# One K for the two lowest score levels, and the first block through two experts before the second

## The chip, the cores and the metric

The kernel runs on one core of one Trainium2 chip. The metric is device microseconds for one execution. TensorE, VectorE, ScalarE and GpSimd are abbreviated PE, DVE, ACT and POOL in the profile, and PEld is TensorE's load of stationary operands. SP is the engine whose queue issues most transfers.

## The reference

A gated linear attention recurrence on 4 batches, 8 heads, 768 tokens and 48 dimensions is followed by a mixture of 4 experts over all tokens, each with two layers (384 to 1024 to 384), weighted by normalised probabilities. All in float32:

```python
for t in range(S):                                   # S = 768, D = 48
    state = alpha[:, :, t, :, None] * state + np.einsum('bhd,bhe->bhde', k[:, :, t], v[:, :, t])
    y[:, :, t] = np.einsum('bhd,bhde->bhe', q[:, :, t], state)
x = y.transpose(0, 2, 1, 3).reshape(B * S, H * D)    # 3072 x 384
p = domain_probs / (domain_probs.sum(-1, keepdims=True) + 1e-09)
for e in range(4):
    out += p[:, e:e + 1] * (np.maximum(x @ w1[e], 0.0) @ w2[e])
```

## The kernel before

**Units and groups.** The tokens are cut into 24 units, each 128 tokens of one batch (`units`). Units 0 and 1 form group 0, then come groups of four units, and the last group has two. For each group all four experts are run over the group's tokens; a unit's place in its group is its slot. `up(gi, e, fc, slots)` is one of eight column tiles of expert e's first layer (line 790 for group 0, line 796 for the others) and `down(gi, e, slots, ...)` is the second layer (line 875). In this text (0, 1) stands for group 0 with expert 1.

**Group 0 works on plain float32 weights.** A matmul in plain float32 leaves two records in the trace. From group 1 on, float32r matmuls are used with the weights split into parts. The splits are made during group 0: `split_piece` (lines 261, 263, 264) rounds a piece on ScalarE, takes the rests on VectorE, and GpSimd's queue writes the parts to `kept` in DRAM (line 268), from where later groups load them. A list `making` says which pieces come next, and `background()` starts one at each of its calls, with at most four under way. Each expert has four pieces (NQ = 4) of 384 KB for each layer. The raw first-layer weights of experts 0 and 2 use one set of tiles, those of experts 1 and 3 another (`shared`); the next expert's are loaded at the middle of `up` of the present expert. The raw second-layer weights of group 0 are loaded into one part of the `hidden` tiles (hT).

**Attention of a unit.** `attention(u)` is a generator; each `yield` ends a step. The steps turn alpha, K and Q (AT, KT, QT: rows are the dimensions of head pairs, columns the 128 tokens). Up to unit 5 this is done on TensorE (`turned`, line 298), from unit 6 on (`in_runs`) by VectorE's transpose (line 499). The rows of the transposed tiles that hold no dimension are set to zero by a scale of 0 or 1 per row, held in the last column of `ident_all`; before, that is an activation on AT (line 503). Then come seven levels: at level li tokens are paired in blocks of m = 1, 2, 4, ... 64; the later block's Q is scored against the earlier block's K, with decay between them. For each level, `copy_q` (line 552, ScalarE, two copies of 64x256) writes the later blocks' Q into one of four tiles `qb`, with the two heads of a pair apart; `next_q` multiplies Q by decay in place (line 559) and joins decays (line 561); `next_k` copies half of K (line 570, ScalarE) and multiplies the other half (line 571). `products` makes a level's scores: 16 matmuls of 32 columns (line 579). `take` writes them into `near` through a mask (line 586). Levels 5 and 6 are `mid` (line 638) and `far` (line 633). Scores are copied to `lat` (lines 650, 653, 658), and `result` makes the unit's output `yps` (line 680). The state is updated through `sps` (line 717).

**Order.** The engines' order is written by hand. While the matmuls of the experts are emitted, `advance(cost)` moves a clock; `waiting` holds steps of units with the clock at which each is due, so the attention of later units stands between the matmuls of earlier ones. `deal()` spreads the steps of units 2 and later over the time by `BEATS`. Unit 0 has a function of its own (`first_unit`), which also runs unit 1's first three steps. Before, the first block, unit 0, goes through expert 0 alone (the loop with `up(0, 0, fc, slice(0, 1))`) while the rest of unit 1's attention is emitted; then unit 1 goes through expert 0, and both units through experts 1, 2 and 3 together.

Of the kernel before, what the change touches and what calls it, by code (L numbers as in the profile page):

```python
# [20 lines left out]
def kernel(  # L21
# [41 lines left out]
    P = 128  # L63
# [74 lines left out]

    blocks = [const.tile([P, NP, 2, HALF], F32, name=f"qb{i}") for i in range(4)]
    free = deque(blocks)  # L140

    def raw(u, nm):
        if nm == "v":
# [26 lines left out]

    def portions(gi, e):
        n = len(groups[gi])
        return [slice(1, n)] if gi == e == 0 else [slice(0, 3), slice(3, n)] if (gi, e) == (1, 0) else [slice(0, n)]

    fresh = lambda gi, e: gi == 1 or (gi, e) == (2, 0)

# [35 lines left out]
    def load_piece(l, i, beside=False, rest=False):  # L212
        if i >= E * NQ * LAST:
            return
        gi, k = divmod(i, E * NQ)
        e, c = divmod(k, NQ)
        if gi > l and not (l == 1 and fresh(gi, e)):
            if l == 0:
                w = wt[l][i] = wts.tile([P, 3, KC * QF], F32R, name="w1", bufs=AHEAD)
                nc.sync.dma_start(out=w.bitcast(F32), in_=kept[l][k])  # L220
                return
            w = second(rest)
            nc.sync.dma_start(out=w.bitcast(F32), in_=kept[l][k][:, 2:] if rest else kept[l][k][:, :2])
            wt[l].setdefault(i, []).append(w)
            return
        if l == 1 and gi == 0 and not beside:
            return
        if l == 0:

            if e == 0:  # L230
                shared[c] = second(True)[:, 0], second(False)[:, 1]
            w = shared[c][e % 2].bitcast(F32)
        else:

            if gi > 0:
                if c == 0:
                    shared["w2"] = hid.tile([P, NQ, KC * QF], F32, name="raw2", bufs=1)
                w = shared["w2"][:, c]
            else:
                w = hidden[c][:, 0].rearrange("p f n -> p (f n)")[:, :KC * QF].bitcast(F32)  # L240
        wt[l][i] = w
        if l == 0:
            nc.sync.dma_start(
                out=w.rearrange("p (c f) -> p c f", f=QF),
                in_=moe_w1[e].rearrange("(c p) f -> p c f", p=P)[:, :, c * QF:(c + 1) * QF])
        else:
            nc.sync.dma_start(
                out=w.rearrange("p (c d) -> p c d", d=DM),
                in_=moe_w2[e].rearrange("(c p) d -> p c d", p=P)[:, c * FPQ:(c + 1) * FPQ])
# [237 lines left out]
    def attention(u):  # L487
# [12 lines left out]

        if u >= in_runs:
            turn("a", AT)
            nc.scalar.activation(out=AT, in_=AT, func=ACT.Copy, scale=ident_all[:, P + QUAD:])
        else:
            nc.scalar.copy(out=AT, in_=turned(pair(ra)))
        after = u + 1 if u > 1 else len(units)
# [17 lines left out]
            own_terms()  # L524
        yield
        load(after, "k")
        if u >= in_runs:
            turn("q", QT)
            nc.vector.tensor_mul(QT, QT, AT)
        else:  # L530
            nc.vector.tensor_mul(QT, turned(pair(rq)), AT)
        if own_late:
            own_terms()
        yield
        load(after, "q")

        decs = [AT]
        KTs = [KT]  # L540
        qbs = []
        spread = lambda t, m: t.unsqueeze(3).broadcast_to([*t.shape, m])
        halved = lambda t: t.rearrange("p a (b two) -> p a b two", two=2)

        def copy_q(li):
            m = LEVELS[li]
            qv = halves(QT, m)[:, :, :, 1, :]
            qb = free.popleft()
            qbs.append(qb)
            for i in range(2):  # L550
                rows = slice(HD * i, HD * (i + 1))
                nc.scalar.copy(out=qb[rows, :, i, :].rearrange("p a (b r) -> p a b r", r=m),  # L552
                               in_=qv[rows])
# [10 lines left out]
        def next_k(li):  # L564
            m = LEVELS[li]
            old = new = halves(KTs[li], m)
            if li + 1 < len(LEVELS):
                KTs.append(keys())
                new = halves(KTs[-1], m)
                nc.scalar.copy(out=new[:, :, :, 1, :], in_=old[:, :, :, 1, :])  # L570
            nc.vector.tensor_mul(new[:, :, :, 0, :], old[:, :, :, 0, :],  # L571
                                 spread(halved(decs[li])[:, :, :, 1], m))

        def products(li, out):
            each = QUAD // 2
            for p in range(NP):
                for s in range(P // QUAD):
                    rows = slice(QUAD * s, QUAD * (s + 1))
                    nc.tensor.matmul(out[rows, 2 * p:2 * p + 2], lhsT=KTs[li][:, p, rows],  # L579
                                     rhs=qbs[li][:, p, :, each * s:each * (s + 1)], start=True, stop=True)  # L580
            free.append(qbs[li])

        def take(li, scores):
# [4 lines left out]
                mk.unsqueeze(1).broadcast_to([P, H, QUAD // (2 * m), m]),  # L588
                scores.rearrange("p a (b r) -> p a b r", r=m))

        def scores(n):
            return ps.tile([P, n, H, QUAD // 2], F32, name="sc", tag="sc")


        for li in range(3):
            copy_q(li)
            next_q(li)
            next_k(li)
            yield
        copy_q(3)  # L600

        nc.vector.tensor_mul(near, ident_all[:, P:P + QUAD].unsqueeze(1).broadcast_to([P, H, QUAD]),
                             dot.unsqueeze(2).broadcast_to([P, H, QUAD]))
        yield
        bank = scores(3)
        for li in range(3):
            products(li, bank[:, li])
        next_q(3)
        next_k(3)
        take(0, bank[:, 0])  # L610
        take(1, bank[:, 1])
        yield
        copy_q(4)
        next_q(4)
        next_k(4)
        take(2, bank[:, 2])
        yield
        copy_q(5)
        next_q(5)
        next_k(5)  # L620
        yield
# [1 line left out]
        if cb > 0:  # L623
            next_q(6)
        yield
        bank = scores(3)
        mid = bank[:, 2].rearrange("p (r i x) n -> p r i (x n)", i=2, x=2)
        far = ps.tile([P, NP // 2, 2, HALF], F32, name="far", tag="sc")

        for r in range(NP // 2):  # L630
            for n in range(P // QUAD):
# [3 lines left out]
        for r in range(NP // 2):  # L635
            for n in range(P // QUAD):
                s, p = n // 2, 2 * r + n % 2
                nc.tensor.matmul(mid[QUAD * n:QUAD * (n + 1), r], lhsT=KTs[5][:, p, HALF * s:HALF * s + QUAD],  # L638
                                 rhs=qbs[5][:, p, :, QUAD * s:QUAD * (s + 1)], start=True, stop=True)
        for li in (3, 4):  # L640
            products(li, bank[:, li - 3])
        free.extend(qbs[5:])
        take(3, bank[:, 0])
        take(4, bank[:, 1])
        next_k(6)
        yield
        parts = lat.rearrange("p (r s i) c -> p r s i c", s=2, i=2)
# [112 lines left out]
    def up(gi, e, fc, slots=None):  # L760
# [2 lines left out]
        begins, ends = lo == 0, hi == n  # L763
        c, f = divmod(fc, FPQ)
        i = first_piece(gi, e) + c
        if fc == 0 and begins:
            for k in range(NQ):
                hidden[k] = hid.tile([P, 2, FPQ, NT], F32R, name="hT", bufs=NQ)
        if gi == fc == 0 and begins:
            for k in range(NQ):  # L770
                load_piece(1, e * NQ + k, beside=True)
        beside = BESIDE[(gi, e) == (1, 0)]
        if fresh(gi, e) and fc in beside and begins:
            making.append(split_piece(1, first_piece(gi, e) + beside[fc]))
        if gi == 0 and e > 0 and fc in SPLIT_AT:
            making.append(split_piece(0, e * NQ + SPLIT_AT[fc]))
        if gi == 0 and e + 1 < E and fc == FCH // 2 and begins:
            for k in range(NQ):
                load_piece(0, (e + 1) * NQ + k)
        col = slice(f * P, (f + 1) * P)  # L780
        if gi > 0:
            w = wt[0][i].rearrange("p t (c f) -> p t c f", f=QF)[:, :, :, col]
        else:
            w = wt[0][i].rearrange("p (c f) -> p c f", f=QF)[:, :, col]
        parts = [hidden[c][:, part, f, lo:hi] for part in range(2)]
        whole = parts[1].bitcast(F32)
        one = ps.tile([P, NT], F32, name="one", tag="g", bufs=4)[:, :hi - lo]
        if gi == 0:
# [35 lines left out]
    def down(gi, e, slots, between):  # L824
# [1 line left out]

        first = first_piece(gi, e)
        tiles = range(FCH)
        if gi == e == slots[0] == 0:
            making.extend(split_piece(0, k) for k in range(NQ))  # L830
        if gi == 0 and e < E - 1 and slots[0] == (e == 0):
            making.extend(split_piece(0, first + NQ + k) for k in range(2))
        if gi == 0 and e == E - 1 and slots[0] == 1:
            making.extend(split_piece(1, first + NQ + k) for k in range(NQ // 2))
# [17 lines left out]
        for n, (slot, part, fc) in enumerate(steps):  # L852
# [12 lines left out]
                    load_piece(1, first + NQ + k)  # L865
            if n == begins[slot]:
                sums[slot] = ps.tile([P, DM], F32, name="ops", tag="g", bufs=4)
            h = hidden[c][:, :, f, slot * P:(slot + 1) * P]
            if part < 3:
                w = ws[c][part // 2].rearrange("p t (c d) -> p t c d", d=DM)[:, part % 2, f]  # L870
                h = h[:, part % 2]
# [96 lines left out]
    with tc.manual_schedule():  # L968
# [4 lines left out]
            for r in (early[nm], apart[nm]):  # L973
                nc.gpsimd.memset(r[:, :, D:], 0.0)
        nc.gpsimd.memset(lat, 0.0)
        for t in values + blocks:
            nc.gpsimd.memset(t, 0.0)
        for t in sts[:-1]:
            nc.gpsimd.memset(t, 0.0)
# [11 lines left out]
        def fill(times, n=P):  # L991
            for _ in range(times):
# [5 lines left out]
        nc.sync.dma_start(out=p_all, in_=moe_domain_probs.rearrange("(n p) e -> p n e", p=P))  # L998

        span = cost(0, 0, 0) * FCH / 2 + cost(1, 0, 0)  # L1000
        waiting.extend((span * (k + 1) / 15, u, runs[u])
                       for k, u in enumerate([1, 1, 1, 0, 1, 0, *[1] * 8]))
        for fc in range(FCH):
            up(0, 0, fc, slice(0, 1))
            if fc == FCH // 2:
                norm_probs()
            advance(cost(0, 0, 0) / 2)
        down(0, 0, [0], deque())
        while waiting:
            next(waiting.popleft()[2], None)  # L1010
        clock = 0.0
        waiting.extend((1.0 + k, 1, runs[1]) for k in range(2))
        waiting.extend(deal())

        for (gi, e), after in zip(tasks, [*tasks[1:], (None, None)]):
            pieces = portions(gi, e)
# [45 lines left out]
```

## Time and profile before

| what | value |
|---|---|
| median of 3 runs | 993.67 us (991.96 to 996.77) |
| profiled execution, its own time | 995.26 us |
| span of the profile | 993.5 us |
| mean granted TensorE clock | 0.993 |
| TensorE busy | 966.4 us (97%) |
| VectorE / ScalarE busy | 545.1 us (55%) / 468.5 us (47%) |
| HBM read, written | 219.69 MB, 42.47 MB |

The chain that ended last is 90% TensorE; the two layers of the experts (lines 875 and 796) make 40% and 37% of the span, the score products of line 579 make 3%. Group 0's experts run from 22.1 us to about 155 us, and the first expert matmuls of group 1 begin at 155.0 us. A busy TensorE in these tables is not TensorE at its peak, and some records of matmuls are missing, so that counts in short stretches can fall short.

### The profile page before, as it was taken

What the parts mean: (1) busy time and instruction counts of PE and PEld (TensorE: products, weight loads), DVE (VectorE), ACT (ScalarE), POOL (GpSimd) and SP (SyncE); (2) the same over time, 40 slices, a digit from 0 to 9 for tenths busy, and PEclk for the clock granted to TensorE, in tenths of its full rate; (3) what the DMA queues carried; (4) which work ended last, traced back from release to release, by engine and by line L of the source; (5) the groups of instructions that cost most, each with busy time, mean ns of one, the idle gap of its engine ahead of it and who ended that gap; (6) DMA issues with size and microseconds to landing.
All of it is one profiled execution on the core that took longest, in us unless ns stands there. A gap on an engine that the chain in (4) does not pass through costs nothing.

```text
span 993.5 us, 26117 instructions
## 1 busy us (share of the span) xinstructions
PE 966.4 (97%) x10988; PEld 860.4 (87%) x10988; DVE 545.1 (55%) x1217; ACT 468.5 (47%) x1106; POOL 47.1 (5%) x95
## 2 busy tenths in 40 slices
PE   8799979999999999999999999999999999999998
PEld 7677658989889889899899898898988999999998
DVE  4676668596866756556545545656666321131312
ACT  4676776584554654445454434555455313111111
POOL 2010000020110200000000000000000000000000
PEclk9999989999999999999999999999999999999999
DMA  9499996899999999978987968988797707272721
GB/s 207 150 336 325 312 356 194 239 315 324 384 305 338 350 311 339 329 275 298 342 256 265 331 221 300 366 273 260 269 312 274 269 2 287 94 288 93 282 99 49
DMA packets 168325, 263.86 MB, mean 266 GB/s; under 512 B 93040, under 2 KB 136432, under 8 KB 155920
## 3 DMA queue, kind: packets, MB, share of 16 engines
q1 hardware_dynamic: 160464, 219.79, 67.7%
q0 software_dynamic: 7296, 42.08, 10.6%
q8 instruction: 86, 1.41, 0.6%
q10 hardware_dynamic: 448, 0.32, 0.1%
q14 instruction: 31, 0.25, 0.1%
HBM read 219.69 MB, written 42.47 MB: 264 GB/s over the span
## 4 chain that ended last, share of the span: by engine, by line
PE 90%; ACT 3%; DMA 2%; DVE 2%; issue 1%; SPq 0%; POOL 0%; DVEq 0%; ACTq 0%; POOLq 0%
PE ops L875 40%; PE one L796 37%; PE yps L680 4%; PE sc L579 3%; PE one L790 2%; DMA w2r<-in_moe_w_dram 2%; PE tp L298 2%; PE far L633 1%; ACT qb L552 1%; PE sps L717 1%; DMA sq<-in_q_dram 1%; PE sc L638 0%; DVE AT L499 0%; PE idle L993 0%; ACT w L261 0%
## 5 line engine op out<-in xcount | busy, mean ns | idle before, releaser
L796 PE MATMUL one<-xT,w 128*128 128x512 f32 (+2 forms) x1512 | 346.9, 385 | 0.0
L796 PEld LDWEIGHTS one<-xT,w 128*128 128x128 f32 x1512 | 274.7, 188 | 52.9 <-issue 0.2
L875 PE MATMUL ops<-w,hT 128*128 128x384 f32 x1408 | 253.9, 338 | 0.0
L798 ACT ACTIVATE hT<-one 128x512 fp32r<-128x512 f32 (+3 forms) x200 | 109.1, 546 | 301.6 <-PE one L796 300.8
L875 PEld LDWEIGHTS ops<-w,hT 128*128 128x128 f32 x1408 | 243.3, 188 | 2.3 <-issue 0.2
L821 DVE SCALAR_TENSOR_TENSOR hT<-one,hT 128x512 fp32r<-128x512 f32 (+3 forms) x200 | 123.7, 626 | 129.4 <-ACT hT L798 128.9
L559 DVE TENSOR_TENSOR QT<-QT,AT 128x256 f32<-128x256 f32 x158 | 67.0, 424 | 153.7 <-ACT qb L552 152.6
L552 ACT COPY qb<-QT 64x256 f32<-64x256 f32 x322 | 130.7, 406 | 16.6 <-PE sc L579 6.6
L875 PE MATMUL ops<-w2r,hT 128*128 128x384 f32 x704 | 127.8, 337 | 0.0
L875 PEld LDWEIGHTS ops<-w2r,hT 128*128 128x128 f32 x704 | 122.2, 188 | 0.3 <-issue 0.2
L896 DVE SCALAR_TENSOR_TENSOR acc<-ops,p_all,acc 128x384 f32<-128x384 f32 x66 | 39.5, 613 | 73.9 <-PE ops L875 73.5
L571 DVE TENSOR_TENSOR KT<-KT,AT 128x256 f32<-128x256 f32 x161 | 67.3, 418 | 0.0
L570 ACT COPY KT<-KT 128x256 f32<-128x256 f32 x138 | 57.6, 417 | 3.3
L586 DVE COPY_PREDICATED near<-masks,sc 128x128 f32<-128x128 uint8 x115 | 40.8, 355 | 27.4 <-PE sc L579 25.8
L579 PEld LDWEIGHTS sc<-qb,KT 128*32 128x32 f32 x3680 | 37.7, 110 | 15.6 <-issue 10.3
L579 PE MATMUL sc<-qb,KT 128*32 128x32 f32 x3680 | 42.3, 198 | 7.1 <-ACT qb L552 3.6
L875 PE MATMUL ops<-hT 128*128 128x384 f32 x128 | 48.0, 522 | 0.0
L905 POOL DMA_DIRECT2D out_dram<-acc x22 | 11.9, 540 | 671.1 <-DVE acc L896 671.1
L561 DVE TENSOR_TENSOR AT<-AT 128x256 f32<-128x256 f32 (+1 forms) x138 | 39.0, 283 | 4.7
L875 PEld LDWEIGHTS ops<-hT 128*128 128x128 f32 x128 | 24.5, 203 | 15.1 <-issue 2.7
L658 ACT COPY lat<-near 32x256 f32<-32x256 f32 x92 | 36.9, 401 | 0.8
L680 PE MATMUL yps<-lat,rv 128*32 128x128 f32 x736 | 33.9, 279 | 2.1 <-ACT lat L658 2.1
(127 smaller groups left out, 783.1 us busy)
## 6 DMA issues: line engine op xcount, KB each, us to landing
w<-kept SPq DMA_DIRECT2D x80, 1152.0 KB, 7.6
w<-kept SPq DMA_DIRECT2D x60, 768.0 KB, 8.1
w2r<-kept SPq DMA_DIRECT2D x60, 384.0 KB, 7.5
kept<-w POOLq DMA_DIRECT2D x16, 1152.0 KB, 8.9
kept<-w POOLq DMA_DIRECT2D x16, 768.0 KB, 13.1
raw<-in_moe_w_dram SPq DMA_DIRECT2D x20, 384.0 KB, 13.1
hT<-in_moe_w_dram SPq DMA_DIRECT2D x16, 384.0 KB, 5.6
kept<-w2r POOLq DMA_DIRECT2D x16, 384.0 KB, 14.2
```

The source lines that it names most:

```text
L552: nc.scalar.copy(out=qb[rows, :, i, :].rearrange("p a (b r) -> p a b r", r=m), in_=qv[rows])
L559: nc.vector.tensor_mul(qv, qv, spread(dv[:, :, :, 0], m))
L570: nc.scalar.copy(out=new[:, :, :, 1, :], in_=old[:, :, :, 1, :])
L571: nc.vector.tensor_mul(new[:, :, :, 0, :], old[:, :, :, 0, :], spread(halved(decs[li])[:, :, :, 1], m))
L579: nc.tensor.matmul(out[rows, 2 * p:2 * p + 2], lhsT=KTs[li][:, p, rows], rhs=qbs[li][:, p, :, each * s:each * (s + 1)], start=True, stop=True)
L586: nc.vector.copy_predicated(near.rearrange("p a (b two r) -> p a b two r", two=2, r=m)[:, :, :, 1, :], mk.unsqueeze(1).broadcast_to([P, H, ...
L680: nc.tensor.matmul(yps[QUAD * j:QUAD * (j + 1), c, :], lhsT=lhsT, rhs=rhs, start=begins, stop=ends)
L796: nc.tensor.matmul(one, lhsT=w[:, part, kc], rhs=x_part(gi, part % 2, kc)[:, lo:hi], start=(part == 1 and kc == 0), stop=(part == 0 and kc ...
L798: nc.scalar.activation(out=parts[0], in_=one, func=ACT.Relu)
L821: nc.vector.scalar_tensor_tensor(out=low, in0=x, scalar=0.0, in1=top.bitcast(F32), op0=ALU.max, op1=ALU.subtract)
L875: nc.tensor.matmul(sums[slot], lhsT=h, rhs=w, start=(n == begins[slot]), stop=(n == ends[slot]))
L896: nc.vector.scalar_tensor_tensor(out=acc, in0=part, scalar=scale, in1=acc, op0=ALU.mult, op1=ALU.add)
```

## The change

Two things are changed.

In `attention`, the mask is applied to Q instead of A: AT is no longer scaled, the copies of Q for level 0 take the scale, and Q times A becomes one instruction with the scale in it. Level 0 is scored with the unscaled Q of the odd tokens against K after level 0's decay, which is the K that level 1 uses too; so level 0's K is updated in place, with no copy. The Q of levels 0 and 1 goes into one new tile `odd`, and one set of 16 matmuls of 64 columns (QUAD = 32 for each of the two heads) makes both levels' scores. Levels 2 and 3 join them in the first scores; the second scores hold `far`, `mid` and level 4 in one bank. The copies of Q for a level are issued at the end of the step before. The number of steps is the same.

In the order of group 0, unit 0 goes through expert 0 and then expert 1, while the rest of unit 1's attention, and the first steps of `deal()`, stand between; then unit 1 goes through experts 0 and 1; experts 2 and 3 run over both. For that, expert 1's raw second-layer weights are loaded in the middle of `up` of expert 0 into the tile `raw2`; expert 1's hidden values for group 0 go into the second half of expert 0's `hidden` tiles; the splits and the load of expert 2's first-layer weights move to the pass in which the expert is last used by `up`.

```diff
 def portions(gi, e):
-        return [slice(1, n)] if gi == e == 0 else ...
+        return [slice(1, n)] if gi == 0 and e < 2 else ...
 # load_piece, second-layer weights
-            if gi > 0:
+            if gi > 0 or e == 1:
 # attention
         if u >= in_runs:
             turn("a", AT)
-            nc.scalar.activation(out=AT, in_=AT, func=ACT.Copy, scale=ident_all[:, P + QUAD:])
...
+        def copy_pairs(src, li):
+            m = LEVELS[li]
+            to = odd.rearrange("p a i (s l b r) -> p a i s l b r", l=2, b=EACH // m, r=m)
+            of = halves(src, m)[:, :, :, 1, :].rearrange("p a (s b) r -> p a s b r", b=EACH // m)
+            for i in range(2):
+                rows = slice(HD * i, HD * (i + 1))
+                nc.scalar.activation(out=to[rows, :, i, :, li], in_=of[rows], func=ACT.Copy,
+                                     scale=pads[rows] if li == 0 and u >= in_runs else 1.0)
 # next_k
-            if li + 1 < len(LEVELS):
+            if li == 0:
+                KTs.append(KT)
+            elif li + 1 < len(LEVELS):
 # steps: Q, then levels 0 to 4
+        if u >= in_runs:
+            turn("q", QT)
+            copy_pairs(QT, 0)
+        else:
+            plain = turned(pair(rq))
+            nc.vector.tensor_mul(QT, plain, AT)
+            copy_pairs(plain, 0)
...
+        if u >= in_runs:
+            nc.vector.scalar_tensor_tensor(out=QT, in0=QT, scalar=pads, in1=AT, op0=ALU.mult, op1=ALU.mult)
+        next_q(0)
+        next_k(0)
+        copy_pairs(QT, 1)
+        yield
+        next_q(1)
+        next_k(1)
+        copy_q(2)
+        yield
+        next_q(2)
+        next_k(2)
+        copy_q(3)
+        yield
...
-        bank = scores(3)
-        for li in range(3):
-            products(li, bank[:, li])
+        products(KTs[1], odd, QUAD, first)
+        level(2, rest[:, 0])
+        level(3, rest[:, 1])
...
 # second scores
-        for li in (3, 4):
-            products(li, bank[:, li - 3])
+        level(4, last)
 # up
-        if gi == 0 and e + 1 < E and fc == FCH // 2 and begins:
+        if gi == 0 and e + 1 < E and fc == FCH // 2 and (ends if e == 1 else begins):
             for k in range(NQ):
                 load_piece(0, (e + 1) * NQ + k)
+            for k in range(NQ if e == 0 else 0):
+                load_piece(1, NQ + k, beside=True)
 # down
-        if gi == e == slots[0] == 0:
+        if (gi, e) == (0, 1) and slots[0] == 0:
             making.extend(split_piece(0, k) for k in range(NQ))
-        if gi == 0 and e < E - 1 and slots[0] == (e == 0):
+        if gi == 0 and e < E - 1 and slots[0] == (e < 2):
             making.extend(split_piece(0, first + NQ + k) for k in range(2))
 # the first block
-        for fc in range(FCH):
-            up(0, 0, fc, slice(0, 1))
-...
-        down(0, 0, [0], deque())
-        while waiting:
-            next(waiting.popleft()[2], None)
-        clock = 0.0
-        waiting.extend((1.0 + k, 1, runs[1]) for k in range(2))
-        waiting.extend(deal())
+        for e in range(2):
+            for fc in range(FCH):
+                up(0, e, fc, slice(0, 1))
+...
+                advance(cost(0, 0, 0) / 2)
+            down(0, e, [0], deque())
+            if e == 0:
+                while waiting:
+                    next(waiting.popleft()[2], None)
+                clock = 0.0
+                last = [(span * (k + 1) / 7, 1, runs[1]) for k in range(6)]
+                last += [(span + 1.0 + k, 1, runs[1]) for k in range(2)]
+                waiting.extend(sorted([*last, *deal()], key=lambda x: x[:2]))
+        while waiting[0][0] < span:
+            next(waiting.popleft()[2], None)
```

## The prediction

> **What bounds the kernel now.** I read the page first, then short stretches, then who waits for whom on TensorE, then the order of time where it waits. The page (engines, slices):
>
> ```profile
> PE 966.4 (97%) x10988; PEld 860.4 (87%) x10988; DVE 545.1 (55%) x1217; ACT 468.5 (47%) x1106; POOL 47.1 (5%) x95
> ...
> PEclk9999989999999999999999999999999999999999
> DMA  9499996899999999978987968988797707272721
> ```
>
> TensorE is busy 97% of 993.5 us, and every stretch of 100 us from 200 to 600 and from 700 to 900 shows it fully busy. There only fewer TensorE microseconds shorten the run. The idle time lies in the first 200 us, and this is what it looks like in stretches of 5 us (columns: span, PE, PEld, DVE, ACT, POOL busy, granted clock, DMA share, GB/s):
>
> ```profile
> 30.00:35.00 5.00, 3.74 (x108) 2.43 (x106) 4.49 (x15) 3.57 (x10) 0.00 (x0) 1.00 0.30 72
> 35.00:40.00 5.00, 3.56 (x102) 2.38 (x102) 1.95 (x5) 3.43 (x10) 0.00 (x0) 1.00 0.01 3
> 40.00:45.00 5.00, 4.01 (x36) 2.75 (x37) 0.87 (x2) 1.39 (x4) 0.67 (x1) 0.66 0.57 236
> ```
>
> From 30 to 45 us neither TensorE nor the DMA engines are full, and the clock falls to 0.66 right behind the idle time. TensorE's waits from 20 to 60 us name the cause:
>
> ```profile
> PE yps L680 <- ACT lat L658: 2.1, 1, 2.1
> PE far L633 <- ACT qb L552: 1.6, 1, 1.6
> PE sps L480 <- ACT AT L476: 1.3, 1, 1.3
> PE tp L298 <- ACT AT L505: 0.7, 1, 0.7
> PE sps L717 <- ACT AT L701: 0.6, 1, 0.6
> PE one L790 <- ACT xT L471: 0.4, 1, 0.4
> ```
>
> All six are unit 1's (or 0's, 2's) attention chain on ScalarE; expert 0 on one block is too little work to cover it. The TensorE timeline gives prices of score products (start, length; two records for a matmul):
>
> ```profile
> 30.55 1.06 PE L579 MATMUL sc<-qb,KT 128*32 128x32 f32 x96
> 31.53 2.20 PE L875 MATMUL ops<-hT 128*128 128x384 f32 x6
> ...
> 35.76 0.41 PE L638 MATMUL sc<-qb,KT 128*32 128x64 f32 x16
> 35.98 0.74 PE L579 MATMUL sc<-qb,KT 128*32 128x32 f32 x64
> 36.65 2.20 PE L875 MATMUL ops<-hT 128*128 128x384 f32 x6
> ```
>
> From start to next start: 48 matmuls of 32 columns take 0.98 us, 32 take 0.67 (20.4 to 20.9 ns each); 8 of 64 columns take 0.22 (27.5 ns). Last, the chain of waits in two places:
>
> ```profile
> 63.29 18.64 DMA w2r<-in_moe_w_dram
> 82.01 0.09 ACT w L261
> ...
> 139.42 1.09 DVE AT L499
> 140.59 0.72 ACT AT L503
> 141.31 0.29 ACT qb L552
> 142.07 0.65 PE far L633 x16
> ```
>
> Expert 2's first weights land 18.6 us after their issue, and a split queued on ScalarE (L261) waits for them. And the next unit's mask (L503) stands in ScalarE's queue, waiting for VectorE's transpose, ahead of the copy that the `far` scores need.
>
> **Fewer score products.** Levels 0 and 1 become 16 matmuls of 64 columns instead of 32 of 32: 16 x 27.5 ns = 0.44 us against 0.67, so 0.22 us less (0.23 by the other row). Moving level 3 to the first bank moves 0.33 us, and adds nothing. All 23 units do it on an engine that is full: 23 x 0.22 = 5.1 us. Bounds: 23 x 0 if 64 columns cost 41.8 ns, twice the 20.9; 23 x 0.33 = 7.7 if they cost the 20.9 of 32. I take 27.5, since it is this very shape. The Trainium skill (TensorEngine Tiling (Array Packing), Instruction Overhead) says that a matmul of one column takes as long as one of some 60 columns; by that rule 64 columns would cost hardly more than 32 and this term would come near 7.7 us. The row L638 against L579 speaks against it: 27.5 ns against 20.9.
>
> **ScalarE and VectorE per unit.** Gone from ScalarE: one KT copy (L570, 0.417 us) in 23 units and the mask (L503, 0.724 us) in 18. The mask goes into two things that run anyway: the level-0 copies (nearest row L552, 0.406 us; with a scale from memory at most half of the 724 - 583 ns between L503 and L701 more each) and the product with Q, which becomes a scalar_tensor_tensor of 128x512 (L821, two operands, 689 ns) instead of L529's 692. So VectorE stays as it is and ScalarE loses about 1 us a unit. In the full stretches that is worth nothing: ScalarE is at 62% or less there. It is worth something where TensorE waits for that queue. After 60 us those are the `far` waits on qb: 2.4 us at 142, 0.9 at 174, 1.9 in two places after 200, together 5.2; the ones at 142, 174, 654 and 686 all have L499 and L503 ahead of the copy. At 142 the clock follows: 0.85, 0.50 and 0.97 in the stretches from 140, 145 and 150 cost (0.15 + 0.50 + 0.03) x 5 = 3.4 us. Upper bound 8.6 us. Against it: ScalarE now waits for the transpose of Q instead of A, two steps later, in front of the lat copies; and the first scores need four levels of the chain instead of three, one more multiply and copy (0.42 + 0.82 us) in units 2 to 5, where TensorE already waits 3.6 us in four places for these copies. Lower bound four times 1.24 us, -5. I take +3 for the first (under half of what is there, since the gaps will lie elsewhere) and -1 for the second: +2.
>
> **First block through two experts.** Expert 1 on block 0 adds 8 x 3 matmuls of 128 columns (about 0.22 us each) and 8 of 384 (0.65): 10.6 us of TensorE work that stands between u1's steps, and is taken out of the later pass. It adds 24 matmuls of 128 columns in place of 256: 48 x 0.223 - 24 x 0.433 = 0.3 us (from 12 records in 1.34 and 6 in 1.30 us in the chain). What can go: the six waits, 6.7 us, and the low clock at 41 us: `yps` there took 1.92 us against 1.01 at 86.85, four `ops` matmul records 2.30 against about 1.4, together 1.8 us. What stays: 0.4 (L471), about 0.6 at the state product, and a new one. In expert 1's second layer, ScalarE has before `yps` one pair of odd copies (0.8), 6 lat copies of far and mid (1.8) and 4 of near (1.6), 4.2 us, from about 43.9 on, while TensorE reaches `yps` six `ops` matmuls later, at about 47.4: about 1 us. Sum: 6.7 + 1.8 - 2.0 - 0.3 = 6.2 us. Bounds: 8.5 - 0.3 = 8.2, and about 3 if ScalarE's queue (26 us full of the 40 from 20 to 60) brings back more than half of it.
>
> On the clock, TensorE: Matmul & The Clock Gate (Trainium skill, Part 1) says that it halves after an idle window of some 3.4 us. The row has the half clock behind gaps of 2.1 us and 2.4 us alone, so shorter gaps count too; by the rule neither 1.8 nor any of 3.4 us would hang on them.
>
> **The queues.** Expert 1's second weights (4 x 384 KB) move up to about 26 us, onto SP's queue behind its first weights. They fill DMA engines that stand at 0.30 and 0.01; expert 1's second layer needs them at about 41, and issue to landing of this kind has a median of 6.2 us: nothing. Behind them on SP stand v of unit 2 and then unit 3's loads, none due before 45. They take some 4.5 us of DMA time (1.5 MB at about 340 GB/s) out of the full stretch after 60 us. Expert 0's split moves with the second layer that hides it, from about 37 to 50 us to about 46 to 53; on POOL's queue its kept writes follow it, and behind them stands nothing until the memsets at 115.8: nothing. The other way goes expert 2's first weights: issued at 63.3 now, 25.6 us before (0,2) starts at 88.9. In the new order the issue is in the second block's pass of expert 1, about 12 us before (0,2) starts, and some 7 us before the first split of them reaches ScalarE. Behind that split stand relu and all copies of units 3 and 4. Cover: unit 3's loads and expert 1's second weights are out of the way by then. Price if it holds: ScalarE's wait was 2.05 us and cost TensorE 0.87; I take 1.5 us. Without cover: see the last rival.
>
> **Sum.** 6.2 + 5.1 + 2.0 - 1.5 = 11.8 us. The profiled execution took 995.26 us (span 993.5 and 1.8 around it), which gives 983.5; the median of the three runs shown is 993.67, 1.6 below it, and 11.8 off that is 981.9. I forecast 982.
>
> **The rivals.** *All waits go*: 8.5 - 0.3 + 5.1 + 8.6 = 21.9 at most; with half of the 8.6 about 17, 976. For it: every stall found sits on ScalarE's queue. Against: 12 us of work compressed into a queue that is three quarters full from 60 to 160. *64 columns at the price of 32*, if the issue of records and not their columns sets the pace: 23 x (0.44 - 0.33) = 2.5 us more, 979.5; L638 speaks against it. The page on array packing named above (Trainium skill) would have it so. *The merged product buys nothing* (64 columns at 41.8 ns): 987. *Expert 2 is late, half way*: TensorE waits about 6 us at (0,2), since landing is 16 to 18.6 us behind the issue again; 989. *Slower*: the same landing, but ScalarE is what stops. The split is queued some 7 us after the issue, so 18.6 us to landing block ScalarE for 11.6 us. TensorE loses 6.4 at (0,2), then some 5 us while the blocked copies are worked off ahead of the relus, and 3.4 of low clock as at 142: 14.8 us against 13.3 gained, 995. With one more turn of that (expert 3's weights, the w buffers that free late) 998. It decides from a first landing over 17 us after issue. For it: today's landings of these four are 16.1 to 18.6 us, beside kept writes of 4.6 MB that are there again. Against: 1.5 MB less in the queue ahead of them.
>
> **How the numbers follow.** Forecast (978 to 986) 0.52, all waits go 0.13, the 32-column price 0.04, merged for nothing 0.06, late half way 0.13, slower 0.12. Range: from 973.5, in the first rival, to 992, above the half-way case; left out are the slower rival and the extreme of the first. What measures as a change is over 0.5% (5 us, 988.7 and 998.6). Faster: 0.52 + 0.13 + 0.04 + 0.06 and half of the half-way case, 0.81. Slower by over 0.5% is the end of the last rival alone, 0.07; the rest, 0.12, is within.
>
> **What would show it.** Right: 16 matmuls of 64 columns in 0.44 us ahead of 32 in 0.67 in each unit's first scores; no `far` or `yps` wait over 1.5 us before 60 and no clock of 0.66 at 40; (0,2) starting at about 81 to 83 instead of 88.9; no wait of L552 behind a masked copy ahead of `far`. Wrong: ScalarE's L261 waiting many us for expert 2's weights at about 75; TensorE idle at the start of (0,2) with low clock behind it; new waits at the first scores of units 2 to 5.

## The result, and the profile after

The changed kernel takes 992.59 us (median of 22 runs, 988.28 to 994.68), the kernel before beside it 995.18. The ratio is 0.997, 95% interval [0.996, 0.998]. It is faster by 0.3%, where 1.2% (982 us) was forecast, and the time lies just above the range. The profiled run has a span of 991.9 us. Its page (engines, granted clock and DMA in slices of 24.8 us):

```profile
PE 968.2 (98%) x10300; PEld 864.0 (87%) x10300; DVE 548.0 (55%) x1217; ACT 458.2 (46%) x1073; POOL 47.4 (5%) x96
...
PEclk9989999999999999999999999999999999999999
DMA  9678998799999999989988978988797707272721
```

688 matmul records are gone, as the change says, and ScalarE is 10.3 us less busy, about half of the 1 us a unit that was forecast. TensorE, however, is not less busy: 968.2 us against 966.4. The stretches of 5 us of the changed kernel (span, PE, PEld, DVE, ACT, POOL busy, granted clock, DMA share, GB/s) show what became of the early idle time:

```profile
40.00:45.00 5.00, 5.00 (x93) 4.44 (x93) 2.41 (x6) 3.44 (x11) 0.00 (x0) 1.00 0.42 82
...
55.00:60.00 5.00, 1.57 (x9) 1.42 (x7) 4.25 (x9) 3.04 (x8) 1.50 (x4) 0.76 0.93 383
60.00:65.00 5.00, 5.00 (x114) 4.76 (x114) 3.12 (x9) 0.30 (x2) 0.11 (x1) 0.56 0.98 389
...
75.00:80.00 5.00, 2.56 (x23) 2.37 (x22) 2.55 (x6) 3.68 (x12) 0.92 (x2) 1.00 1.03 373
80.00:85.00 5.00, 4.20 (x23) 3.61 (x24) 2.48 (x5) 4.19 (x12) 0.53 (x1) 0.66 0.99 418
```

From 40 to 45 us TensorE is now full and its clock is 1.00 (before: 4.01 us busy, clock 0.66). That much went as forecast. But two new holes stand at 55 and 77 us, each with a stretch of half clock: from 57.5, while the first hole still lasts, to 64.4, and from 81.4 to 84.9. TensorE's waits from 50 to 100 us (total, times, longest, in us) name what it waited for in these holes:

```profile
PE sps L737 <- ACT AT L721: 3.4, 1, 3.4
PE one L814 <- ACT hT L816: 2.4, 1, 2.4
PE ops L900 <- ACT hT L816: 0.7, 1, 0.7
```

The chain that ended last from 48 to 62 us (start, us, what) shows what ScalarE was late for:

```profile
52.69 0.47 DVE w L264
53.16 0.87 DVE w L265
54.02 0.47 DVE w L264
54.49 0.87 DVE w L265
55.36 0.34 DVE near L619
55.70 0.34 DVE QT L558
...
57.21 0.84 ACT w L262
58.05 0.48 ACT AT L721
...
58.58 2.02 PE sps L737 x8
```

The lines `w L264`, `w L265` on VectorE and `w L262` on ScalarE are the splits of expert 0's weights. On VectorE two of them (2.7 us) run ahead of a query product (`QT L558`); ScalarE's copies wait 1.66 us for that product, and the fourth split (`w L262`) stands ahead of the turned keys (`AT L721`) that TensorE needs for the state product. At 77 us it is the same with expert 1's splits.

Measured by the starts of each unit's output product (`yps`) against before: unit 2 is 4.3 us late, unit 3 5.8, unit 6 1.7, unit 17 1.3; unit 20 is 1.4 us early and the last one 1.9. The second block's pass of expert 2 starts at 93.16 us, where 81 to 83 was forecast and before had 88.88.

### The profile page after: what moved, and what is told of

Read it like the earlier page. It is cut to its first block, busy times and chain, and to the rows that moved or that the text cites. A ratio compares the mean times of both kernels' runs of the same rounds, so it can differ in the third digit from the quotient of the medians.

```text
span 991.9 us, 24647 instructions
## 1 busy us (share of the span) xinstructions
PE 968.2 (98%) x10300; PEld 864.0 (87%) x10300; DVE 548.0 (55%) x1217; ACT 458.2 (46%) x1073; POOL 47.4 (5%) x96
## 4 chain that ended last, share of the span: by engine, by line
PE 91%; ACT 4%; DMA 2%; DVE 1%; issue 1%; SPq 0%; POOL 0%; DVEq 0%; POOLq 0%; ACTq 0%
PE ops L900 40%; PE one L820 37%; PE yps L700 4%; PE sc L579 3%; PE one L814 2%; PE tp L299 2%; PE sc L655 1%; DMA rq<-in_q_dram 1%; PE sps L737 1%; ACT odd L542 1%; DMA w<-kept 1%; PE sc L660 0%; ACT lat L673 0%; ACT w L262 0%; PE idle L1018 0%
## 5 line engine op out<-in xcount | busy, mean ns | idle before, releaser
L551 ACT COPY qb<-QT 64x256 f32<-64x256 f32 x230 | 92.5, 402 | 38.2 <-DVE QT L558 36.4
L558 DVE TENSOR_TENSOR QT<-QT,AT 128x256 f32<-128x256 f32 x158 | 66.5, 421 | 59.4 <-ACT qb L551 42.2
L542 ACT ACTIVATE odd<-QT,ident 64x256 f32<-64x256 f32 x36 | 18.8, 522 | 70.9 <-DVE QT L500 70.7
L571 ACT COPY KT<-KT 128x256 f32<-128x256 f32 x115 | 47.1, 410 | 2.1
L900 PE MATMUL ops<-hT 128*128 128x384 f32 x96 | 36.0, 514 | 0.0
L820 PE MATMUL one<-KT,w 128*128 128x256 f32 x288 | 34.6, 279 | 0.0
L820 PEld LDWEIGHTS one<-KT,w 128*128 128x128 f32 x288 | 34.4, 188 | 0.0
```

The costliest lines, as they stand in the source:

```text
L558: nc.vector.tensor_mul(qv, qv, spread(dv[:, :, :, 0], m))
L820: nc.tensor.matmul(one, lhsT=w[:, part, kc], rhs=x_part(gi, part % 2, kc)[:, lo:hi], start=(part == 1 and kc == 0), stop=(part == 0 and kc ...
L900: nc.tensor.matmul(sums[slot], lhsT=h, rhs=w, start=(n == begins[slot]), stop=(n == ends[slot]))
```

## The experiments

Each ratio is to the kernel before on the same chip, with its 95% interval.

**e1, the attention part alone** (the mask with Q, the paired levels, four levels in the first scores). Against the change, the first block, its loads and its splits are put back as before:

```
-        for e in range(2):
-            for fc in range(FCH):
-                up(0, e, fc, slice(0, 1))
+        for fc in range(FCH):
+            up(0, 0, fc, slice(0, 1))
...
+        down(0, 0, [0], deque())
```

> Only the attention part: mask with Q, levels 0 and 1 on one K, four levels in the first scores; group 0 in the order of before. Theory A (the order part lost what the attention part gained): the product of levels 0 and 1 saves little (from the changed kernel's trace the pair takes 0.47 us, and a 32-column level in the middle of a set only 0.28 us, so about 0.05 to 0.1 us a unit, 1 to 2 us in all), but the waits of TensorE behind the masked copy go (2.4 us at 142 with its low clock, 0.9 at 174, 1.9 after 200): 6 to 9 us less than before, 986 to 989. Theory B (the attention part itself makes the new waits in the first 100 us, since ScalarE now waits for Q and four levels stand before the first scores): no faster than before, waits of several us before 100 us.

Measured: 985.62 us, 0.9908 [0.9893, 0.9924]. The attention part alone is worth 9.2 us, over three times the whole change. Against before, its `yps` starts are level up to unit 4, then 5.3 us early at unit 5, level again from there (6.0 at unit 9, 6.4 at unit 17), and gain another 4.1 by the last. So it does not gain evenly, as fewer matmuls would, but in a few places where before has waits: 133 to 165 us and 601 to 706 us.

**e2, the order part alone** (first block through two experts, with its loads and splits). Against the change, all of the attention is put back as before:

```
-        products(KTs[1], odd, QUAD, first)
-        level(2, rest[:, 0])
-        level(3, rest[:, 1])
+        bank = scores(3)
+        for li in range(3):
+            products(li, bank[:, li])
...
```

> Only the order part: the first block through two experts, then the second; attention as before. Theory A: the waits near 55 and 77 us and the low clock behind them are there as in the changed kernel, (0, 2) starts 3 to 5 us later than at 88.9, and the total is 3 to 6 us above before, 998 to 1001. Theory B: the first 100 us are about 6 us shorter, (0, 2) starts near 83, total near 989.

Measured: 994.65 us, 0.9998 [0.9986, 1.0009]: no difference, which neither theory had. The waits of before in 20 to 60 us are mostly gone, and new ones (1.4 for turned keys, 1.7 for the sequencer, 1.5 and 1.2 for `hT`) stand from 54 to 86.

**e3, expert 0's splits one slot earlier**, on the whole change, so that they are through before unit 2's copies come:

```
-        if (gi, e) == (0, 1) and slots[0] == 0:
+        if gi == e == slots[0] == 0:
```

> The changed kernel with expert 0's four splits asked for at the second layer of expert 0 on the first block, as before the change, not at expert 1's. Theory A (the splits stand in VectorE's and ScalarE's queues ahead of unit 2's copies and unit 1's turned keys): the wait of 3.4 us at 55 and the 3.4 us of low clock from 57 to 64 go, about 6 us less than the changed kernel, 986 to 987. Rival C (these queues are full whatever the order): the wait comes back earlier or later in the first 70 us, less than 2 us gained.

Measured: 989.11 us, 0.9937 [0.9923, 0.995], 3.5 us less than the change by the medians, where about 6 were expected. The wait for turned keys and the low clock at 57 us are gone; the wait of 2.4 us behind expert 1's splits stays, at 72 us, with its low clock.

**e4, the 3.4 us hole filled**: five matmuls on zeros ahead of unit 1's state product, on the whole change:

```
+            if u == 1:
+                z = sts[B - 1].rearrange("p a i d -> p (a i d)")
+                for _ in range(5):
+                    nc.tensor.matmul(sps.rearrange("p a i d -> p (a i d)"), lhsT=z[:, :P], rhs=z,
+                                     start=True, stop=True)
```

> The changed kernel with five matmuls on zeros (128x384, some 3.2 us) put on TensorE's queue just ahead of unit 1's state product, where it waits 3.4 us; they write the tile that the product then overwrites. If the low clock from 57.4 to 64.2 us comes from that wait: clock full there, about 3 us less than the changed kernel, although nothing waits less. If a wait of 3.4 us has nothing to do with it: the clock is low all the same, no gain.

Measured: 990.36 us, 0.9961 [0.9946, 0.9976]; its span is 987.0. The interval overlaps that of the change, so the time alone shows little, but the stretches show the clock (the columns as above):

```profile
55.00:60.00 5.00, 4.79 (x117) 3.64 (x116) 4.43 (x11) 2.52 (x7) 1.07 (x2) 1.00 1.04 406
60.00:65.00 5.00, 5.00 (x35) 4.09 (x34) 3.35 (x9) 3.50 (x11) 0.00 (x0) 1.00 1.02 404
```

No useful work was added, and yet the clock is 1.00 where the change has 0.76 and 0.56. Here the low clock came from TensorE's idle time, not from the load on the chip.

**e5, expert 1's splits spread too**: e3, and expert 1's four splits asked for one by one over expert 0's pass on the second block:

```
+        if gi == e == 0 and ends and fc % 2 == 0:
+            making.append(split_piece(0, NQ + fc // 2))
-        if gi == 0 and e < E - 1 and slots[0] == (e < 2):
+        if gi == 0 and 0 < e < E - 1 and slots[0] == (e < 2):
```

> The kernel with expert 0's splits early, and expert 1's four splits asked for one by one at the first layer of expert 0 on the second block, instead of two at its second layer and two at expert 1's. Theory A (where a split stands in the queues decides): the wait of 2.4 us near 72 and the low clock behind it go, 3 to 4 us less than with the early splits of expert 0 alone, 985 to 986. Theory D (the DMA engines, full from 90 to 160 us, set the pace there, so that what is gained before 90 is given back): unit 2's output comes 3 us or more earlier, unit 4's at about 133 as in every kernel so far, total within 1.5 us of 989.

Measured: 983.82 us, 0.9903 [0.9885, 0.9921]. Both holes are gone, and units 2 to 4 are 4.2 to 5.0 us early where the change has them 4.3 to 5.8 late. This version beats both kernels; it is not told apart from e1.

**e6 and e7, a third of the kept first-layer bytes**, to test whether the DMA engines set the pace. In e6 (on e3) and e7 (on e1) only one of three parts of a first-layer split is written, and read three times; the other two are left out, so the output is not the reference's:

```
-                nc.sync.dma_start(out=w.bitcast(F32), in_=kept[l][k])
+                nc.sync.dma_start(out=w.bitcast(F32), in_=kept[l][k][:, :1].broadcast_to([P, 3, KC * QF]))
...
+                if l == 0:
+                    nc.gpsimd.dma_start(out=kept[l][k][:, :1], in_=w[:, :1].bitcast(F32))
+                    continue
```

> The kernel with expert 0's splits early, and of each split first-layer piece one part of three written to DRAM; later groups load that part three times (its output is not the reference's). 12.6 MB less written during group 0, as many loads and the same work on all engines. Theory D: unit 4's output comes 3 us or more before 133, the wait of ScalarE for expert 3's weights (2.9 us) goes, total 4 us or more below 989. Theory E (ScalarE's and VectorE's queues in their order set the pace from 90 to 155): less than 1.5 us.

> The attention part alone, with the same cut of what is written (its output is not the reference's). Theory D: the same gain of several us against 985.6. Theory E: less than 1.5 us. If only the early-split order gains, the DMA engines bind in the new order alone.

Measured: 987.04 us, 0.9933 [0.9909, 0.9956], and 985.42 us, 0.9903 [0.9875, 0.993]: no different from 0.9937 and 0.9908. The DMA engines did become freer (from 100 to 120 us their share is 0.57 in e6 against 1.01 in e3, and 0.41 in e7 against 0.84 in e1). So the DMA theory falls as far as these writes go: they do not set the time.

**e8, the mask alone**: before, with the mask moved into the product with Q.

```
-            nc.scalar.activation(out=AT, in_=AT, func=ACT.Copy, scale=ident_all[:, P + QUAD:])
-            nc.vector.tensor_mul(QT, QT, AT)
+            nc.vector.scalar_tensor_tensor(out=QT, in0=QT, scalar=ident_all[:, P + QUAD:], in1=AT, op0=ALU.mult, op1=ALU.mult)
```

> The kernel before with one edit: the mask goes from A (the activation, 18 units) into the product with Q; all levels as before. If the masked copy ahead of the copy for far was what TensorE waited for: 5 us or more of the 9 us of the attention part, 987 to 990, no far wait at 142 and after 600. If the shorter K chain and the four levels in the first scores did it: 2 us or less.

Measured: 990.45 us, 0.9973 [0.996, 0.9987], 2.7 us less than before, between the two expectations. Its `far` wait near 142 us fell from 2.4 to 0.3 us, but nothing came of it there. TensorE's waits from 60 to 200 us of e8:

```profile
PE sc L579 <- issue: 4.4, 1, 4.4
```

Before has 2.2 us in that line. In both, TensorE goes on at 145.7 to 145.9 us. In both it stops after the same 58 of the set's 64 records, and the profile names nothing that it waits for. Most likely it is its own code: a queue named "instruction" moves 16 KB packets, one of them at 143.2 us (before) and 143.4 (e8), taking 1 us, while the DMA engines are at 1.01. This is inferred from the times, not shown. The gain of e8 comes later, from the `far` waits at 174 us and at 654 and 686.

**e9 and e11, the code shifted**: is part of e1's gain a matter of where the 16 KB packets end? Before (e9) and e1 (e11) with more start-up filling:

```
-        fill(7)
+        fill(5)
+        fill(32, 8)
```

> The kernel before, with 30 tiny matmuls added to its start-up filling, where TensorE has nothing else to do: some 120 more instructions, half a 16 KB block of instructions, and no other change. Theory: the waits of TensorE's sequencer at 143 us (2.2 us) and 606 us (1.3 us) hang on where a block's border falls in its program, and a border within a set of score products under full DMA costs the wait and the low clock behind it. Then these waits go or move to other places: 3 to 7 us less than before (987 to 991 us), or as much more if new borders fall in worse places. Rival: the waits come from the DMA traffic or from the order of the engines at that time: same places, no difference beyond 0.15%.

> The attention part alone (which took 985.6 us), with the same 30 tiny matmuls in its start-up filling. Theory: its gain rests partly on where the blocks' borders fall, since it has 1470 instructions fewer; shifted by half a block, a wait of the sequencer can come back with a low clock behind it: up to 5 us more, about 990 us. Rival: the gain is the removed work on ScalarE and in the products, whatever the borders: 985 to 986.5 us.

Measured: 1002.58 us, 1.0076 [1.0061, 1.009], and 997.28 us, 1.0028 [1.0015, 1.0041]. My price for the filling was wrong: each of the 60 added records took 0.21 us, with 8 columns as with 128, and the first `yps` came 9.0 and 9.6 us later. Beside that, e9 won 1.6 us back at 606 us, where before waits 1.3 us in the same way. Near 145 us that wait was gone too, but the way from unit 4 to unit 5 got no shorter (31.2 us, before 31.1): the wait for the copied queries was 2.8 us instead of 2.4, and TensorE waited 2.4 us more for VectorE's part of group 1's input (`xT`), with half clock behind it, which before does not.

**e10, first scores later in each unit's order**, on e5:

```
-    BEATS = [0.04, 0.08, 0.12, 0.18, 0.24, 0.3, 0.355, 0.4, 0.46, 0.52, 0.58, 0.635, 0.68, 0.74, 0.85, 1.0, 1.01]
+    BEATS = [0.04, 0.08, 0.12, 0.18, 0.24, 0.3, 0.355, 0.44, 0.48, 0.52, 0.58, 0.635, 0.68, 0.74, 0.85, 1.0, 1.01]
```

> The change with expert 0's splits early and expert 1's splits spread (983.8 us), with the first scores placed later in each unit's order (shares 0.40 and 0.46 to 0.44 and 0.48). Theory: the remaining waits of first score products for the copied keys and turned queries (2.5 us in all) come from four levels being due there too early: 1 to 2.5 us less, 981.5 to 983 us. Rival: the later first scores push the weights and the unit's output later, and as much waiting appears ahead of the output product: 983.5 to 985.5 us.

Measured: 989.11 us, 0.9948 [0.9931, 0.9964], by the ratios 4.5 us more than e5 (0.0045 x 994.6); the theory and its rival both missed. TensorE's waits from 60 to 200 us of e10:

```profile
PE sc L655 <- ACT qb L551: 7.3, 4, 3.1
```

The waits of the first scores (2.5 us) went, and three times as much came back at the second scores, whose copies now had less time.

**e12 and e13, a smaller shift**: before (e12) and e1 (e13) with

```
-        fill(7)
+        fill(2)
+        for _ in range(30):
+            nc.tensor.matmul(idle[:64, :32], lhsT=zeros[:64, :64], rhs=zeros[:64, :32], start=True, stop=True)
```

> The kernel before, with five of its seven start-up fillings (some 2.4 us) replaced by 30 small matmuls of 64x64 on 64x32 (0.02 to 0.06 us each by the score products' rows, 0.6 to 1.8 us): the borders of the instruction blocks move, without the 9 us of start-up that the larger filling cost. Theory: the waits of TensorE's sequencer for instructions at 143 us (2.2 us) and 606 us (1.3 us) go or move; the earlier shift got 1.6 us back at 606 and nothing at 143, where another wait (2.8 us for turned queries) took the place: 1.5 to 2 us less than before. Rival: borders in new bad places: same or up to 3 us more.

> The attention part alone (985.6 us) with the same small filling. If its gain is the removed work on ScalarE and the cheaper way through unit 4, it keeps 985 to 987 us, ratio 0.990 to 0.992. If 3 to 5 us of it were luck with the blocks' borders (shifted by the larger filling, the attention part gained 5.3 us and not 9.1), 988 to 990 us, ratio 0.994 to 0.996.

Measured: 997.37 us, 1.0023 [1.0009, 1.0037], and 992.51 us, 0.9974 [0.9963, 0.9986]. This filling was not free either: 60 records in 6.6 us, so 0.11 us each on one tile of the array, and the first `yps` 4.4 and 5.9 us late. But the two pairs agree: e11 is 5.3 us below e9, and e13 4.9 below e12, where e1 is 9.2 below before. About 5 us of the attention part stay when the code and the start are shifted, and about 4 do not.

**e14, the order part alone with e5's splits** (e2 with the edits of e3 and e5).

> The order part alone (994.7 us, ratio 0.9998), with expert 0's splits asked for one slot earlier and expert 1's spread over expert 0's second pass. Theory: the order part pays what was forecast for it (6.2 us by its length of cover) once the splits are out of the way of the copies: 986 to 989 us, ratio 0.991 to 0.994. Rival: with both parts and these splits the time was 983.8, only 1.8 us below the attention part alone, so the order itself is worth 2 us at most, since the units ahead of 133 us are set by the copies and DMAs in either order: 991 to 993.5 us, ratio 0.996 to 0.998.

Measured: 990.01 us, 0.9944 [0.9928, 0.9959], against 0.9998 for e2. It lies just outside the 986 to 989 us of the theory and clear of the rival's ratios. Units 2 to 4 are 4.3 to 4.6 us early, expert 2's pass starts at 84.30 us, and where the change has clock 0.56, e14 has (the columns as above):

```profile
60.00:65.00 5.00, 5.00 (x28) 3.53 (x27) 4.71 (x12) 4.24 (x11) 0.74 (x2) 1.00 1.09 375
```

## Why the prediction was wrong, by its steps

**First block through two experts, 6.2 us: the mechanism right, its cover wrong.** Of the six waits only `yps` (1.5 us in the change) and the one of 0.4 us (now 1.0) are left before 50 us, the low clock at 41 us went, and with the splits out of the way the order part is worth 4.9 us (e14, by the medians; 5.6 by its ratio). In e14 the added waits come to more than the 1.3 us that are missing: `yps` 1.8 us where I had 1.0, and 0.9 and 0.7 for `hT` that I had not. The step that failed is a sentence under "The queues": I moved expert 0's splits "from about 37 to 50 us to about 46 to 53" and named POOL's queue behind them, and then wrote "nothing". Their own engines were left out. A split is 1.3 us on VectorE and 0.84 on ScalarE; four of them were put ahead of unit 2's products and copies and of unit 1's turned keys. The price can be read off between e14 and the change. The hole at 55 us is 3.4 us. Of the 6.8 us of half clock that begin in it, 5.8 lie behind it and cost half, 2.9. The `hT` waits are 1.5 us longer (2.4 and 0.7 against 0.9 and 0.7). Of the 3.4 us of half clock from 81.4, 2.7 lie outside a wait and cost 1.4. Together this is 9.2 us. The `yps` starts of units 2 and 3 differ by 8.9 and 10.4. e3 takes the first half of it away, e5 all.

**Expert 2's weights late, 1.5 us, and two rivals built on it: did not happen.** They are issued from 71.31 us on, land 4.6 to 6.6 us later, where the rivals needed 16 to 18.6, and the first is split at 90.1 without a wait. The long landing came one expert later: expert 3's first weights took 17.2 us, and ScalarE waited 2.2 us for them, at 114 us, without a wait of TensorE behind it. I looked for the blocked queue at expert 2 and it was at expert 0, with the same signs (ScalarE's splits, then low clock).

**Fewer score products, 23 x 0.22 = 5.1 us: mis-sized, about 1 us.** The TensorE timeline of the changed kernel has the new sets (start, length, records):

```profile
297.82 0.65 PE L579 MATMUL sc<-odd,KT 128*32 128x64 f32 x32
298.29 0.74 PE L579 MATMUL sc<-qb,KT 128*32 128x32 f32 x64
...
312.07 0.41 PE L660 MATMUL sc<-qb,KT 128*32 128x64 f32 x16
312.29 0.48 PE L579 MATMUL sc<-qb,KT 128*32 128x32 f32 x32
```

The pair of levels takes 0.47 us to the next start, near the forecast 0.44. But what it replaces was not worth 0.67. In the second scores, where one level went, the last row takes 0.41 us to the next start (312.70) with 32 records and took 0.67 to 0.68 with 64: one 32-column level costs 0.27 us at the margin, and a set ends with some 0.14 us that belongs to no level. Two levels are 0.54, the pair 0.47: 0.07 us, not 0.22. I had divided whole sets by their matmuls and so taken the tail for part of each matmul's price. Two sets of before against two of after agree: 0.98 + 1.36 against 1.17 + 1.09 us, 0.08 less. And `yps` of e1 gains 0.4 us from unit 9 to unit 17, 0.05 a unit; 23 units make some 1 to 2 us. The bounds (0 to 7.7) held it, and the rival "the merged product buys nothing" was nearer for this term. The rule of the Trainium skill on array packing (TensorEngine Tiling (Array Packing), Instruction Overhead), taken as a price in these float32 sets, is not borne out either: 16 matmuls of 64 columns cost 0.47 us where 16 of 32 cost 0.27.

**ScalarE relief, 2 us: low.** ScalarE has 12.1 us less to do in e1 (456.4 against 468.5), half a us a unit where about one was forecast, and VectorE, forecast to stay as it is, has 3.0 more (548.1 against 545.1). What this is worth in time came out higher. The mask alone gives 2.7 (e8). The whole attention part gives 9.2, of which some 1 to 2 is the products, but only about 5 us stay when code and start are shifted (e9 against e11, e12 against e13). The feared cost of four levels in the first scores is there, 2.5 us of waits in the change, but before has 3.6 us in the same kind of line: it is nothing new.

**The sum.** With the splits moved, the change gives 983.8 us, close to the 982 forecast, but by other terms. That it came so near is luck. Attention part and order part do not add: by the medians 9.3 + 4.9 would be 14.2, and e5 has 9.7. From unit 4 to unit 5 e1 gains 5.1 us and e5 3.5. There e5 still has a gap of 1.9 us at 143.7 with half clock behind it, e1 one of 1.5 at 148.0 without. From unit 17 to the last, e1 gains 4.1 us, e14 1.6 and e5 only 3.1: the wait of 1.3 us that before has at 606 is gone in e1 and in e14 and so counted twice, and e5 has one of 0.9 us for copied keys there. The rest of the difference was not tracked down.

**Open.** Which part of the 4 us that the attention part loses when shifted hangs on the borders of the code packets, and which on the later start, is not settled: both fillings moved both. They also ran in a slow start-up: four turning records behind them still take 0.86 us (at 19.18 in e9, at 11.08 in e12), where before has 0.47 from 6.91 on. Before swallowed 2.6 us of the small filling's delay by unit 2, and e1 0.6.

## What to carry to other kernels

When work is moved to cover one stall, follow every instruction it brings along on its own engines, not only its DMAs: what runs next on each queue is what will be late. Price a small matmul by the difference of two sets of different length, never by a set divided by its count. A gain read from an early stall should be tried with the start shifted by a few us, since half of it may hang on where things happen to fall.

## What the runs showed of the hardware

- TensorE's clock is granted in stretches of 3.41 us. In all 16 traces the half clock lasts one or two of them, and starts a whole number of them after the first clock record (in the change at 57.55, 81.45, 112.17 and 156.54 us, that is 7, 9 and 13 stretches apart). Filling the hole kept the clock full (e4). What decides is how busy TensorE was in the stretch before: each of the 42 times that the clock fell, apart from the end of the run, this was 0.21 to 0.51 of it. From 0.47 to 0.51 the clock also stayed full nine times, and from 0.53 on always. So a gap counts by how it lies to these stretches. In e14 a gap of 2.83 us from 134.95 is shared by two of them and the clock stays, while one of 2.39 us from 147.24 falls into one and the clock halves (the columns as above):

```profile
133.15:136.57 3.42, 1.80 (x6) 0.76 (x4) 2.94 (x7) 0.51 (x2) 0.00 (x0) 1.00 1.01 426
136.57:139.98 3.41, 2.20 (x99) 1.90 (x100) 2.19 (x5) 3.12 (x8) 0.00 (x0) 1.00 1.00 421
...
146.81:150.22 3.41, 0.99 (x3) 0.48 (x4) 2.27 (x6) 3.33 (x9) 0.00 (x0) 1.00 0.99 412
150.22:153.63 3.41, 3.41 (x13) 3.32 (x14) 3.38 (x8) 1.36 (x4) 0.54 (x1) 0.50 1.09 312
```

  The Trainium skill (TensorE: Matmul & The Clock Gate, Part 1) has an idle window of about 3.4 us. The length agrees with these traces, but TensorE need not be idle all through it: here about half of it was enough.
- TensorE can stop with nothing in the profile to wait for, most likely for its own code: 2.2 us in before and 4.4 in e8 near 143 us, when a 16 KB packet is fetched while the DMA engines are full and the score products use up instructions fast (192 matmul and weight-load records in about 1 us).
- At the start of an execution, a matmul on a full 128x128 weight tile took 0.21 us a record with 8 columns (e9), as much as a turning one of 128 columns behind it (0.86 us for four), and one of 64x64 on 64x32 repeated on the same tile 0.11 (e12). Turning records later take half of that (0.44 us for four), so the price of such a filling later on is not shown. In the score sets, spread over the array, a record takes about 0.01 us.
